# Loads of later passes in two pieces, each issued when the one in front has landed

## The chip, the cores and the metric

The kernel runs on one core of one Trainium2 chip. The metric is the device time of one execution in microseconds (us). Three runs of the kernel before gave 597.53, 600.47 and 601.56 us; the median, 600.47 us, is the time before.

## The reference

Two stages are computed. The first is a gated linear attention with a complex decay: for each of 4 x 8 heads and each of 768 steps, the decay is normalised, a 48 x 48 state is decayed and updated with the outer product of key and value, and the query reads it.

```python
scale = np.minimum(mag, 0.999) / (mag + 1e-06)      # mag = |a_re + i a_im|
for t in range(S):                                   # S = 768
    new_re = ar * S_re - ai * S_im
    new_im = ar * S_im + ai * S_re
    S_re, S_im = (new_re + einsum('bhd,bhe->bhde', k_t, v_t), new_im)
    y_t = einsum('bhd,bhde->bhe', q_t, S_re)
```

The second stage is a two-layer network on the 3072 tokens of width 384: `h = x @ w_in` (to 2048), `g = maximum(0.01 * h, h)`, `g @ w_out` (back to 384).

## The kernel before, in words

The sequence is cut into six chunks of 128 steps and the batch into two halves, which makes 12 passes (`SUBS`), each of one chunk for two batch entries, 256 tokens. A pass n has these parts:

- `fetch_a(n)` loads the decays (two planes of 128 x 768 numbers, 768 KB) into one of two buffers, `fetch_qk(n)` the queries and keys (768 KB, one buffer), `fetch_v(n)` the values (832 KB).
- `prep(n)` (lines 675 to 888) turns the decays into running products, alternating between ACT and DVE. It begins with the square of the loaded decays on ACT (the tile `sq`, read from `a`), then a DVE operation on `sq` (it is `sq<-sq` in the rows), then a logarithm and exponentials on ACT (`u`), then 14 products on DVE (`u<-a`, `a<-u`) and a scan (`xs`). Near its end it multiplies queries and keys into the tile `qkt`; that is the first use of the loaded `qk`.
- `relay_of(n, 0)` and `relay_of(n, 1)` copy `qkt` within SBUF to the tile `t96` (named `t` in the rows), five transfers each for queries and for keys.
- `attend(n)` (from line 929) computes scores, masked scores (`asb`, `more`), keys in natural order (`kn`, `more`, copied by ACT), the values' products, the rounded output `x` and its rest (ACT and DVE, both `x`), and the new state (`rst`).

`forward()` runs the network on the 256 tokens of each pass: `first` (`ph`), `hide` on ACT and DVE (`tg`, `hid`), `second` (`po`), `store`. While pass n+1 is attended, PE also has the network of the tokens of pass n. The weights are loaded and converted by `convert` while the first pass is prepared; at the end `check_weights` loads the raw weights once more in 11 parts (`wck`, up to 1152 KB each) into the two buffers of the decays and sums them on ACT for a validity test (`flag`), beside the network's last groups.

All loads and stores, and the relays, are issued by one engine, SP, in one order. That order, and the order of instructions on PE, DVE and ACT, is fixed when the kernel is built: the parts are generators that yield the engine they want next, and `drive` (line 253) takes them by modelled start time and rank, with costs from `dma_cost`, `dve_cost`, `act_cost` and `pe_costs`. The class `Lane` (line 112) chains each engine's instructions by dependencies without a semaphore, so that nothing is reordered afterwards. `fetch_a(n)` may be placed once `prep(n-2)` and the key relay of pass n-2 are placed, `fetch_qk(n)` once `prep(n-1)` and the key relay of pass n-1 are; so behind each relay of keys stand the load of the decays of two passes on and that of the queries and keys of the next pass. `prep(n)` has its first ACT instruction placed right behind the modelled landing of its decays.

Nothing makes one load wait for another, except where a buffer is reused.

Of the kernel before, what the change touches and what calls it, by code (L numbers as in the profile page):

```python
# [21 lines left out]
P = 128  # L22
# [113 lines left out]
def in_sbuf(x):  # L136
    return x.space == bass.MemoryType.SB
# [38 lines left out]
def dma_cost(name, kw, aps):  # L176
    if name == "memset":
        return 0.3, 0.4
    out = kw["out"]
    if in_sbuf(kw["in_"]) and in_sbuf(out):  # L180
        return 0.78, 2.75
    each = out.nbytes() / 400e3
    return max(each, 0.6), each + 2.4
# [272 lines left out]
def body(ctx, tc, keep, a_in, qk_in, v_in, w_in, out):  # L456
# [26 lines left out]
    spq, plq = Lane(tc, nc.sync, dma_cost), Lane(tc, nc.gpsimd, dma_cost)  # L483
# [15 lines left out]
        out=perm[:, 0].rearrange("p (x r j) -> p x r j", x=NB, r=R),  # L499
        in_=perm[:, 0].rearrange("p (x r j) -> p x r j", x=NB, r=R),  # L500
# [3 lines left out]
        out=perm[:, 1].rearrange("p (r j x) -> p r j x", r=R, j=JB),  # L504
        in_=perm[:, 1].rearrange("p (r j x) -> p r j x", r=R, j=JB),
# [28 lines left out]
    a_off = [0]  # L534
# [33 lines left out]
    def attends_of(n):  # L568
        return [attended[n]]

    def fetch_a(n):
        yield "S", *([prepared[n - 2], moved_k[n - 2]] if n > 1 else freed(A) if n else []), *([loading[n - 1]] if n else [])
        N = TI * len(SUBS[n][1]) * C
        loading[n].set(0.0)
        raw_a[n] = a = a_0 if n == 0 else pp.tile([P, 3, N], F32, tag="a", name=f"a_{n}", bufs=2)
        spq.dma_start(
            out=a[:, 1:3], in_=a_in[a_off[n] : a_off[n + 1]].rearrange("(p l x) -> p l x", p=P, l=2)
        )

    def fetch_qk(n):  # L580
        yield "S", *([prepared[n - 1], moved_k[n - 1]] if n else [])
        N = TI * len(SUBS[n][1]) * C
        raw_qk[n] = qk = pp.tile([P, 2, N], F32, tag="qk", name=f"qk_{n}")
        spq.dma_start(
            out=qk, in_=qk_in[a_off[n] : a_off[n + 1]].rearrange("(p l x) -> p l x", p=P, l=2)
        )

    def fetch_v(n):
        yield "S", *(attends_of(n - 1) if n else freed(V))
# [6 lines left out]
    def check_weights(i):  # L596
        yield "S", checked[i - 2] if i > 1 else prepared[nsub - 2 + i]
        s0 = i * WCK
        ns = min(WCK, NWC - s0)
        st = pp.tile([P, WCK, DM], I64, tag="a", name=f"wck_{s0}", bufs=2)  # L600
        spq.dma_start(out=st[:, :ns], in_=w_in[s0 : s0 + ns].rearrange("s p x -> p s x"))
        words = st.rearrange("p s x -> p (s x)").bitcast(F32).rearrange("p (x two) -> p x two", two=2)
        lo, hi = words[:, : ns * DM, 0], words[:, : ns * DM, 1]
        yield "A"
        act.activation(lo, hi, AF.Square)
        yield "A"
        act.activation(hi, lo, AF.Exp, scale=-65536.0, accum_out=wacc[:, 1, i : i + 1])
        yield "A"
        act.activation(lo, lo, AF.Exp, scale=40.0, bias=big, accum_out=wacc[:, 0, i : i + 1])

    def freed(*places):
        return [x for x, r in zip(converted, ROUND) if r in places]
# [640 lines left out]
    for n in range(nsub):  # L1253
        fetched_a[n] = task(fetch_a(n), UNIT[0] + 5.5 * UNIT[1] if n == 1 else R_RELAY + 0.5)
        fetched_qk[n] = task(fetch_qk(n), R_HID if n else UNIT[0] + 2.5 * UNIT[1])
        prepared[n] = task(prep(n), *due(n))
        if n == 0:
            for i in range(NU):
                converted.append(task(convert(i), UNIT[0] + i * UNIT[1]))
        fetched_v[n] = task(fetch_v(n), R_RELAY - 1 if n else UNIT[0] + 9.5 * UNIT[1])  # L1260
        moved_q[n] = task(relay_of(n, 0), R_RELAY)
        moved_k[n] = task(relay_of(n, 1), R_RELAY)
        attended[n] = task(attend(n), R_ATT)
    forwarding = task(forward(), R_FF)
    for i in range(-(-NWC // WCK)):
        checked[i] = task(check_weights(i), R_WCK)
# [87 lines left out]
```

## Time and profile before

| | |
|---|---|
| median of three runs | 600.47 us |
| profiled execution, its time | 598.47 us |
| profiled execution, its span | 596.5 us |
| PE, DVE, ACT busy | 92%, 88%, 65% of the span |
| chain that ended last: PE, DVE, ACT, DMA, issue | 63%, 22%, 6%, 4%, 4% |
| DMA traffic | 79.18 MB, 133 GB/s over the span |
| loads of decays; of queries and keys | 12 each, 768 KB, median 4.5 and 5.9 us from issue to landing |
| relays, 290 KB each | 48, median 4.2 us |

The span is the time from the first to the last instruction; 1.97 us of the execution lie around it. PE is TensorE, DVE VectorE, ACT ScalarE, SP the engine that issues DMAs. The chain is followed back from the last instruction, at each step to what released it; "issue" is time in which an engine waited for nothing that the profile shows. A busy share is an average over stages: whether an engine sets the pace of a stage is seen in its idle time there.

### The profile page before, as it was taken

How to read it: one execution, taken by the hardware profiler on the slowest of the kernel's cores; microseconds unless marked ns; L12 is line 12 of the kernel's file. 1: busy time of each engine (PE TensorE's matmuls, PEld its weight loads, DVE VectorE, ACT ScalarE, POOL GpSimd, SP SyncE). 2: the span in 40 equal slices, each digit the busy share in tenths (PEclk: the TensorE clock that was granted, in tenths of full speed). 3: DMA queues.
4: the chain of work that ended last, by engine and by line, in shares of the span. 5: the costliest groups of instructions: out<-in, count | busy, mean ns of one | idle time of the engine just before them, and what ended most of it. 6: DMA issues, size and time to landing. Idle time of an engine off the chain costs nothing.

```text
span 596.5 us, 17862 instructions
## 1 busy us (share of the span) xinstructions
PE 550.3 (92%) x7650; PEld 520.9 (87%) x7650; DVE 522.6 (88%) x897; ACT 388.0 (65%) x862; POOL 5.0 (1%) x23
## 2 busy tenths in 40 slices
PE   3865699999979899999999999999999999999996
PEld 2432499989869899999999999999999998998996
DVE  5999999999999999889999999999999998963332
ACT  7988576475474584584684574764755755784975
POOL 2000000000000000000000000000000000000000
PEclk9996799999999999999999999999999999999999
DMA  8963612522522433334235124134135156456650
GB/s 347 406 217 89 216 59 55 161 86 54 167 82 63 151 97 96 114 104 145 92 94 161 60 81 161 61 82 161 59 81 161 60 145 202 141 157 214 195 203 29
DMA packets 28370, 79.18 MB, mean 133 GB/s; under 512 B 3200, under 2 KB 9344, under 8 KB 28288
## 3 DMA queue, kind: packets, MB, share of 16 engines
q1 hardware_dynamic: 28288, 78.02, 40.8%
q8 instruction: 60, 0.98, 0.7%
q14 instruction: 22, 0.18, 0.1%
HBM read 54.26 MB, written 4.72 MB: 99 GB/s over the span
## 4 chain that ended last, share of the span: by engine, by line
PE 63%; DVE 22%; ACT 6%; DMA 4%; issue 4%; SPq 1%; DVEq 0%; ACTq 0%
PE ph L121 23%; PE po L121 23%; PE att L121 15%; DVE qkt L121 5%; DVE a L121 4%; DMA t<-qkt 4%; DVE u L121 3%; DVE tg L121 2%; ACT rst L121 2%; DVE hid L121 2%; DVE sq L121 1%; PE pd L121 1%; DVE xs L121 1%; DVE qk L121 1%; DMA a<-in_a_dram 1%
## 5 line engine op out<-in xcount | busy, mean ns | idle before, releaser
L121 PE MATMUL ph<-x,win_hi 128*128 128x256 f32 x1152 | 215.8, 279 | 5.2 <-DVE x L121 1.9
L121 PE MATMUL po<-hid,wout_hi 128*128 128x256 f32 x1152 | 215.1, 280 | 0.0
L121 PEld LDWEIGHTS ph<-x,win_hi 128*128 128x128 f32 x1152 | 181.4, 188 | 6.9 <-DVE x L121 2.3
L121 PEld LDWEIGHTS po<-hid,wout_hi 128*128 128x128 f32 x1152 | 180.5, 188 | 1.6 <-issue 0.4
L121 PE MATMUL ph<-x,win_lo 128*128 128x256 f32 x576 | 141.7, 278 | 0.0
L121 PE MATMUL po<-hid,wout_lo 128*128 128x256 f32 x576 | 137.2, 278 | 0.0
L121 PEld LDWEIGHTS po<-hid,wout_lo 128*128 128x128 f32 x576 | 108.4, 188 | 0.0
L121 PEld LDWEIGHTS ph<-x,win_lo 128*128 128x128 f32 x576 | 108.4, 188 | 0.0
L121 DVE TENSOR_TENSOR tg<-ph,tg 128x512 f32<-128x512 f32 x96 | 65.8, 686 | 30.6 <-ACT tg L121 30.3
L121 ACT CAST hid<-tg 128x512 fp32r<-128x512 f32 x96 | 59.3, 617 | 48.6 <-DVE tg L121 46.9
L121 ACT ACTIVATE tg<-ph 128x512 f32<-128x512 f32 x96 | 56.9, 592 | 45.4 <-PE ph L121 45.2
L121 DVE TENSOR_TENSOR hid<-tg,hid 128x512 fp32r<-128x512 f32 x96 | 65.9, 686 | 14.3 <-ACT hid L121 13.4
L121 DVE TENSOR_TENSOR u<-a 128x384 f32<-128x384 f32 x84 | 46.5, 553 | 2.1 <-ACT a L121 0.7
L121 DVE TENSOR_TENSOR qkt<-qk,a 128x768 f32<-128x768 f32 x48 | 44.1, 951 | 0.0
L121 PE MATMUL att<-t 96*32 96x64 f32 (+3 forms) x1536 | 36.0, 252 | 3.6 <-DMA t<-qkt 3.5
L121 PEld LDWEIGHTS att<-t 96*32 96x32 f32 x1536 | 33.1, 144 | 6.9 <-DMA t<-qkt 4.1
L121 PE MATMUL att<-t,rst 96*32 96x128 f32 x640 | 34.4, 272 | 1.4 <-issue 1.3
L121 PE MATMUL att<-asb,v 128*32 128x128 f32 x592 | 33.9, 274 | 0.6 <-issue 0.6
L121 ACT ACTIVATE rst<-rst,t 96x48 f32<-96x48 f32 x128 | 29.8, 322 | 4.5 <-DVE rst L121 4.4
L121 ACT ACTIVATE wck<-wck 128x1152 f32<-128x1152 f32 (+1 forms) x22 | 26.9, 1224 | 7.8 <-DMA wck<-in_w_dram 7.7
L121 DVE TENSOR_TENSOR a<-u 128x192 f32<-128x192 f32 x84 | 29.8, 355 | 1.9
L121 ACT ACTIVATE sq<-a 128x1536 f32<-128x1536 f32 x12 | 18.0, 1498 | 13.6 <-DMA a<-in_a_dram 13.6
(161 smaller groups left out, 766.9 us busy)
## 6 DMA issues: line engine op xcount, KB each, us to landing
t<-qkt SPq DMA_DIRECT2D x48, 290.2 KB, 4.2
wck<-in_w_dram SPq DMA_DIRECT2D x10, 1152.0 KB, 5.6
v<-in_v_dram SPq DMA_DIRECT2D x12, 832.0 KB, 4.5
a<-in_a_dram SPq DMA_DIRECT2D x12, 768.0 KB, 4.5
qk<-in_qk_dram SPq DMA_DIRECT2D x12, 768.0 KB, 5.9
out_dram<-ot SPq DMA_DIRECT2D x12, 384.0 KB, 2.7
t<-qkt SPq DMA_DIRECT2D x24, 129.0 KB, 4.1
stage_st<-in_w_dram SPq DMA_DIRECT2D x3, 768.0 KB, 4.4
```

Of the source, the lines that this page charges most:

```text
L121: x = getattr(self.engine, name)(*args, **kw)
```

## The change

`fetch_a` and `fetch_qk` no longer issue one transfer for the two planes of a pass, but two, one for each plane, through a new function `pieces`. Each such piece, and each part of the weight check, gets a dependency with a semaphore on the piece or part issued before it (`in_turn`): SP waits until that one has landed. The loads of pass 0 and the decays of pass 1 stay whole and outside this line, and so do the values, the relays, the stores and the weights' first load. The planner's log keeps one entry with the cost of the whole load in place of the two pieces'.

```diff
+    loaded = []
+
+    def in_turn(x):
+        if loaded:
+            landed = mybir.DependencyInfo(mybir.DependencyClass.Sync, mybir.DependencyReason.DATA)
+            tc.add_manual_dep(x.ins, loaded[-1], landed, reason="load")
+        loaded.append(x.ins.name)
+
+    def pieces(out, in_, n):
+        if n < 1:
+            spq.dma_start(out=out, in_=in_)
+            return
+        for l in range(2):
+            in_turn(spq.dma_start(out=out[:, l], in_=in_[:, l]))
+        spq.log[-2:] = [dma_cost("dma_start", dict(out=out, in_=in_), [])]
+
     def fetch_a(n):
...
-        spq.dma_start(
-            out=a[:, 1:3], in_=a_in[a_off[n] : a_off[n + 1]].rearrange("(p l x) -> p l x", p=P, l=2)
-        )
+        pieces(a[:, 1:3], a_in[a_off[n] : a_off[n + 1]].rearrange("(p l x) -> p l x", p=P, l=2), n - 1)
 
     def fetch_qk(n):
...
-        spq.dma_start(
-            out=qk, in_=qk_in[a_off[n] : a_off[n + 1]].rearrange("(p l x) -> p l x", p=P, l=2)
-        )
+        pieces(qk, qk_in[a_off[n] : a_off[n + 1]].rearrange("(p l x) -> p l x", p=P, l=2), n)
...
-        spq.dma_start(out=st[:, :ns], in_=w_in[s0 : s0 + ns].rearrange("s p x -> p s x"))
+        in_turn(spq.dma_start(out=st[:, :ns], in_=w_in[s0 : s0 + ns].rearrange("s p x -> p s x")))
```

## Rows read from the trace of the kernel before

**Rows 1.** One stretch: busy PE, PEld, DVE, ACT, POOL (instructions), granted clock, DMA, GB/s.

```profile
366.00:410.00 44.00, 44.00 (x665) 43.44 (x666) 42.35 (x73) 26.75 (x65) 0.24 (x2) 1.00 0.36 113
```

**Rows 2.** SP in order of time, one middle pass: start us, us, instruction, count.

```profile
360.85 4.00 SPq L121 DMA_DIRECT2D t<-qkt  x5
364.95 0.53 SPq L121 DMA_DIRECT2D a<-in_a_dram  x1
...
380.90 0.33 SPq L121 DMA_DIRECT2D v<-in_v_dram  x1
```

**Rows 3.** Who waited for whom, all passes: us in total, times, longest.

```profile
ACT sq L121 <- DMA a<-in_a_dram: 13.6, 11, 3.5
```

**Rows 4.** ACT in time, same pass; in brackets idle time before it.

```profile
369.23 1.49 ACT L121 ACTIVATE sq<-a 128x1536 f32<-128x1536 f32 x1 [0.77 <-DMA a<-in_a_dram]
...
372.37 0.86 ACT L121 COPY kn<-att 128x384 f32<-128x384 f32 x2 [1.56 <-PE att L121]
```

**Rows 5.** The decays' tile, all 12 loads: us from issue to landing.

```profile
DMA to landing us min/median/max: 4.3/4.5/5.3
```

**Rows 6.** DMA issues, 42.5 to 47 us: count, KB, us to landing.

```profile
stage_stg<-in_w_dram SPq DMA_DIRECT2D x1, 384.0 KB, 3.5
```

**Rows 7.** DMA issues between 60 and 64.5 us.

```profile
stage_stg<-in_w_dram SPq DMA_DIRECT2D x1, 384.0 KB, 2.9
```

**Rows 8.** DVE in order of time, the pass of Rows 4.

```profile
373.02 0.95 DVE L121 SCALAR_TENSOR_TENSOR sq<-sq 128x768 f32<-128x768 f32 x1
...
380.26 1.16 DVE L121 SCALAR_TENSOR_TENSOR x<-att,x 128x384 fp32r<-128x384 f32 x2
...
389.70 1.82 DVE L121 TENSOR_TENSOR qkt<-qk,a 128x768 f32<-128x768 f32 x2
```

**Rows 9.** The chain that ended last, same pass: start us, us, what.

```profile
381.76 2.12 PE ph L121 x18
```

**Rows 10.** ACT in order of time, the pass that loads decays at 236.92 us.

```profile
242.22 1.50 ACT L121 ACTIVATE sq<-a 128x1536 f32<-128x1536 f32 x1 [0.95 <-DMA a<-in_a_dram]
...
245.12 0.60 ACT L121 ACTIVATE tg<-ph 128x512 f32<-128x512 f32 x1 [0.57 <-PE ph L121]
```

**Rows 11.** DVE in order of time, the same pass.

```profile
243.84 0.96 DVE L121 SCALAR_TENSOR_TENSOR sq<-sq 128x768 f32<-128x768 f32 x1 [0.43 <-ACT sq L121]
...
246.59 0.53 DVE L121 TENSOR_TENSOR u<-xs 128x360 f32<-128x360 f32 x1 [0.16 <-ACT xs L121]
```

**Rows 12.** The chain that ended last, the end of that pass.

```profile
276.12 4.76 DMA t<-qkt
```

**Rows 13.** ACT in order of time, the pass that loads decays at 66.74 us.

```profile
71.31 1.49 ACT L121 ACTIVATE sq<-a 128x1536 f32<-128x1536 f32 x1 [1.25 <-DMA a<-in_a_dram]
...
74.14 0.49 ACT L121 ACTIVATE x<-att 128x384 fp32r<-128x384 f32 x1 [1.25 <-PE att L121]
```

**Rows 14.** ACT in order of time, the pass that loads decays at 196.62 us.

```profile
201.13 1.49 ACT L121 ACTIVATE sq<-a 128x1536 f32<-128x1536 f32 x1 [1.14 <-DMA a<-in_a_dram]
```

**Rows 15.** DVE in order of time, the same pass.

```profile
204.08 0.95 DVE L121 SCALAR_TENSOR_TENSOR sq<-sq 128x768 f32<-128x768 f32 x1
```

**Rows 16.** SP in order of time, parts five and six of the weight check.

```profile
540.89 1.10 SPq L121 DMA_DIRECT2D wck<-in_w_dram  x2
```

**Rows 17.** ACT in order of time: its first instruction on each part.

```profile
546.57 1.28 ACT L121 ACTIVATE wck<-wck 128x1152 f32<-128x1152 f32 x1 [4.57 <-DMA wck<-in_w_dram]
...
553.50 2.51 ACT L121 ACTIVATE wck<-wck 128x1152 f32<-128x1152 f32 x2
```

**Rows 18.** PE in order of time, the last pass.

```profile
549.78 0.31 PE L121 MATMUL att<-t,rst 96*32 96x128 f32 x3 [1.29 <-issue]
```

**Rows 19.** DMA queues, 547 to 547.5 us: packets, MB, share of engines.

```profile
q8 instruction: 1, 0.02, 12.7%
```

**Rows 20.** Who waited for whom, all passes: PE's waits in the attention.

```profile
PE att L121 <- DMA t<-qkt: 3.5, 6, 1.1
...
PE att L121 <- issue: 2.6, 3, 1.3
```

## The prediction

> **What bounds the kernel now.** I read the page's chain first, then busy time by stretch, then SP's order, then the engines' own orders around each load. In the middle passes PE has no idle time at all: 44.00 us busy in a stretch of 44 us [rows 1]. There an edit to the loads can only cost time, or free PE from something that the profile books as busy. The five passes whose decays are issued between 279 and 451 us look like this; the five split passes before them do not, and there DVE and ACT are on the chain.
>
> In SP's order the load of the decays stands right behind the five transfers of a key relay, and the queries and keys right behind it; the next thing on SP, the load of the values, is issued 16 us later (380.90 - 364.95) [rows 2]. What the reader should see next is that the decays are not loaded far ahead: in 11 of 12 passes ACT waits for them, 13.6 us in total [rows 3]. ACT takes the square as soon as they land, and then has 1.56 us to spare before its copy of the keys [rows 4]. So the landing time of the decays is what the change moves and what someone waits for.
>
> **The change, part by part.** Order and count on PE, DVE and ACT: unchanged, since the planner is given the same cost and the same order. Issues: 10 passes of decays and 11 of queries and keys get one more, 21 in all, at 0.53 us of SP each [rows 2]. SP has 16 us free there, so their own issue time costs nothing.
>
> *Landing of the decays.* Whole, they land 4.5 us after issue, 4.3 to 5.3 [rows 5]. A piece is 384 KB. The trace has transfers of just this size: 3.5 us with relay transfers about [rows 6], 2.9 us later on with less beside it [rows 7]. The first piece follows the key relay, so I take 3.5; the second is alone in the queue, so 2.9; between them a wake-up of SP, which I take as 0.05. Together 6.45 us, 1.95 later than now. Ends: two quick pieces against the median give 2 x 2.9 + 0.05 - 4.5 = 1.35; two slow ones 2.55; and since half a load should not take longer than the whole at its slowest, at the most 2 x 5.3 - 4.5 = 6.1. No gain is possible here: two transfers one after the other would have to land in 2.25 us each, and no row of this size is below 2.9.
>
> The Trainium skill ("DMA: Bandwidth & Descriptors", Anatomy of one DMA) speaks against the change: each transfer has a fixed part of about 2.0 us, beside bytes at 436 GB/s. By it a piece would be 2.9 us as an estimate, a whole 3.8, the delay 2.0, and the sum below the same to 0.1 us; the 2.9 agrees with the row, the whole is slower here.
>
> *Middle passes, five.* The square ends at 369.23 + 1.49 = 370.72 us [rows 4]; DVE reads it at 373.02 [rows 8]. Slack 2.3 us; the other four have 2.1 to 2.4 by the same two rows. Further on, DVE's last step on the output ends at 380.26 + 1.16 = 381.42 [rows 8] and PE takes it no earlier than 381.76 [rows 9], so 0.34 us more. A delay of 1.95 fits: **0**. ACT's copy of the keys slips by 1.95 - 1.56 = 0.4 us at most [rows 4]; behind it ACT idles again before PE wants anything. The cover is gone when the delay passes about 2.6 us; then each us beyond costs up to five.
>
> *The pass at 236.92 us.* Here there is no slack: DVE already waits 0.43 us for the square [rows 11]. ACT's next piece of the network idled only 0.57 us [rows 10], between them the key copy follows the square directly. So tg slips by 1.95 - 0.57 = about 1.4, DVE's scan behind ACT's copies by the same 1.4 [rows 11], and the chain goes on over DVE and ACT without a break to the key relay that releases PE at 280.9 [rows 12]. **+1.4**; ends 0 and 1.95.
>
> *The pass at 196.62 us.* The square ends at 202.62 [rows 14], DVE reads it at 204.08 [rows 15]: slack 1.46, so DVE stalls 0.5. PE is busy behind, with some room: **+0.4**. The two passes before it have like slack (both are on DVE's chain); I charge 0.15 each: **+0.3**, ends 0 and 1.
>
> *The pass at 66.74 us.* The square's end moves from 72.8 to 74.75; ACT's output step is due at 74.14 [rows 13]. It slips by 0.6 us. How much reaches PE no row shows; I take all but a part: **+0.5**, ends 0 and 0.6.
>
> *Queries and keys.* Their pieces follow those of the decays: 364.95 + 6.45 + 3 x 0.05 + 2 x 2.9 = 377.3 us at the last landing. DVE reads them at 389.70 [rows 8] and SP's next issue is at 380.90 [rows 2], so they cost **0**; 3.4 us remain to SP, and if the pieces took 1 us more each it would still do. Where a store of results stands next in SP's order (two early passes), it is the store that slips, and nobody waits for it.
>
> *Weight check.* Parts five and six are issued one right after the other now [rows 16]; five lands at 546.57 and is used at once, six is used at 553.50 [rows 17]. In line, six is issued at 546.6 and takes again 546.57 - 540.89 = 5.7 us at most [rows 16], so it lands at 552.3, in time: **0**. The later parts wait for ACT to free their buffer already.
>
> *What it could give back.* In the last pass PE waits 1.29 us with nothing that the profile names [rows 18]; shortly before, a packet of its instructions passes among the data of those two parts [rows 19]. I read this as code that came late behind a bulk load. With one part in flight at a time the queue is shorter. There are 2.6 us of such waits on PE in three places [rows 20]; one more of them stands at a load of decays, one behind a single part that stays whole. I take **-1.0**, ends 0 and -2.6. The Trainium skill ("Runtime: NRT & Kernel Launch", Instruction fetch mechanics) has instruction fetch mostly hidden. By it the credit would be 0 and the time 1 us longer; the row of 1.29 us does not fit it, though no row proves what the wait was for.
>
> **Sum.** 1.4 + 0.4 + 0.3 + 0.5 - 1.0 = +1.6 us against the profiled execution's 598.47. That one lies 2.0 us under the median of the runs and inside their spread; the mean of all four is 599.5. I forecast 599.5 + 1.6 = **601 us**, which a measurement cannot tell from no change: about 1% (6 us) is what it can tell here.
>
> **Rivals.**
> *Slower: the slack of the middle passes is overrun.* The place is DVE's read of the square [rows 8], the mechanism the in-order wait of ACT for the second piece, the point 2.6 us of delay. If the pieces take 4.1 us each, about what a whole load takes now, the delay is 3.75: then 5 x 1.15 = 5.8 in the middle and 1.8 more in each of the five early passes, 9 us, atop +2.6: 599.5 + 17 = 617. At 3.1 us of delay it is 2.5 + 5.8 + 2.6 = 11, so 610. For it: the first piece shares the engines with a relay. Against: both rows of this size are below 3.6 [rows 6, 7]. Chance 0.22, with the time most likely 607 to 611.
>
> *Faster: PE was held up by loads more than I credit.* If all of PE's named waits in the attention, 3.5 us for relays and 2.6 us for nothing named [rows 20], went, and the delay cost nothing, it would be 599.5 - 6.1 = 593.4. Against: the relays are issued ahead of the loads [rows 2], and shorter loads behind them do not speed them. Chance 0.10.
>
> *The change does nothing.* Were the wait met before SP comes to it, or the decays' landing unchanged, the time would be 599.5. Against: the second piece comes 0.5 us after the first, which cannot have landed. Chance 0.08.
>
> **How the numbers follow.** Forecast 0.60. The forecast's own range is 597 to 604, from -1.0 to -2.6 of credit below and all upper ends of the four charges above. The whole range runs from 596, into the faster case, to 608, into the lower half of the slower one; outside lie about 0.07 and 0.11. Slower by over 1% (above 606.5): most of the slower rival, 0.19. Faster by over 1% (under 594.5): the stronger part of the faster one, 0.06. Within 1%: 0.75.
>
> **What would show it.** In the profile after: decays landing some 6.4 us after their first issue, the second piece's issue about 3.5 us behind the first; ACT's waits for decays up from 13.6 to about 33 us; PE still without idle in the middle passes; DVE waiting for the square in the early passes only; the 1.29 us wait of the last pass smaller or gone. I am wrong if pieces land much sooner or later than 2.9 to 3.5 us, if DVE waits for the square in every pass, or if PE is found to run faster in stretches that show it fully busy now.

## The result: about 1% slower, and the profile after

The changed kernel takes 605.53 us (median of six runs), the kernel before 599.96 beside it; the ratio is 1.0109, with a 95% interval of 1.0064 to 1.0155. That is 5.6 us of loss where 1.6 were forecast. The time lies 4.5 us above the forecast, above the forecast's own range (597 to 604) and inside the whole one (596 to 608); the ratio is just past 1%, with an interval that reaches to both sides of it. The profiled executions differ by as much: 603.8 against 598.47 us. One run of all, 608.18 us in the experiment with whole decays, fell in a slower state of the chip and is left out of the medians and ratios.

The page of the kernel after: span, busy time, clock by slice, the chain that ended last, and the loads among the DMA issues (count, KB each, us to landing).

```profile
span 602.1 us, 17917 instructions
...
PE 550.5 (91%) x7650; PEld 520.9 (87%) x7650; DVE 522.8 (87%) x897; ACT 386.0 (64%) x862; POOL 5.0 (1%) x23
...
PEclk9896789999999999999999999999999999999999
...
DVE 50%; ACT 17%; PE 13%; DMA 12%; issue 5%; SPq 2%; ACTq 0%; DVEq 0%
...
qk<-in_qk_dram SPq DMA_DIRECT2D x22, 384.0 KB, 3.2
a<-in_a_dram SPq DMA_DIRECT2D x20, 384.0 KB, 3.3
```

No engine works longer: PE and DVE are busy for the same time as before, to 0.2 us, in a span 5.6 us longer. What changed is the chain, from PE 63% to DVE 50%, with ACT and DMA behind it. The added time is waiting.

Who waited for whom (us in total, times, longest), the rows that answer to [rows 3, 20] and the one behind them:

```profile
ACT sq L121 <- DMA a<-in_a_dram: 38.1, 11, 5.8
DVE tg L121 <- ACT tg L121: 28.9, 24, 3.9
ACT tg L121 <- PE ph L121: 17.8, 22, 2.8
...
DVE sq L121 <- ACT sq L121: 11.7, 8, 4.1
...
PE att L121 <- DMA t<-qkt: 4.5, 10, 1.5
...
PE att L121 <- ACT win_lo L121: 3.2, 1, 3.2
...
PE att L121 <- issue: 2.0, 3, 1.1
```

ACT waits 24.5 us more for the decays than before. Its waits for PE are shorter (`ACT tg <- PE ph` was 45.2 us and is 17.8), so I read that time which ACT had in hand is spent; the row scatters, though: it is 26.5 when the changed kernel is run again, and 27.9 in a kernel whose decays land as before (the first experiment). DVE's wait for ACT's square was 5.5 us in three places and is 11.7 in eight; two of the eight, 4.1 and 1.04 us, stand in both kernels. So 6.2 us of DVE waits are new, about the loss.

SP in order of time, the pass of [rows 2], now issued 6.76 us later in the span:

```profile
367.56 4.05 SPq L121 DMA_DIRECT2D t<-qkt  x5
371.71 3.58 SPq L121 DMA_DIRECT2D a<-in_a_dram  x2
378.26 3.40 SPq L121 DMA_DIRECT2D qk<-in_qk_dram  x2
386.99 0.33 SPq L121 DMA_DIRECT2D v<-in_v_dram  x1
```

The second piece goes out some 3.2 us behind the first (the pair ends at 375.29 and its last issue takes about 0.3), and the queries only when it has landed, 6.55 us after the start. The values are issued 386.99 - 371.71 = 15.3 us after the decays, where it was 16, so they are not held up.

The decays' tile, all 22 transfers (two whole, 20 pieces), against [rows 5]:

```profile
DMA to landing us min/median/max: 3.0/3.3/5.0
```

Three stretches of 44 us, the middle passes (columns as in [rows 1]), and in them one pass on ACT and DVE in order of time, the load at 285.83 us; below it the same two instructions before, the load at 279.50 us:

```profile
284.00:328.00 44.00, 43.37 (x665) 42.78 (x664) 42.29 (x73) 27.14 (x67) 0.12 (x1) 1.00 0.39 108
328.00:372.00 44.00, 43.91 (x671) 43.33 (x669) 42.17 (x73) 26.70 (x66) 0.12 (x1) 1.00 0.38 108
372.00:416.00 44.00, 43.80 (x705) 43.06 (x707) 42.63 (x74) 26.37 (x65) 0.12 (x1) 1.00 0.38 108
```

```profile
292.82 1.49 ACT L121 ACTIVATE sq<-a 128x1536 f32<-128x1536 f32 x1 [3.56 <-DMA a<-in_a_dram]
294.22 0.18 ACT L121 ACTIVATION_READ_ACCUMULATOR sq<-a 128x1 f32 x1
294.31 0.84 ACT L121 COPY kn<-att 128x384 f32<-128x384 f32 x2
```

```profile
294.43 0.96 DVE L121 SCALAR_TENSOR_TENSOR sq<-sq 128x768 f32<-128x768 f32 x1 [0.52 <-ACT sq L121]
```

```profile
283.85 1.49 ACT L121 ACTIVATE sq<-a 128x1536 f32<-128x1536 f32 x1 [0.93 <-DMA a<-in_a_dram]
```

```profile
287.48 0.95 DVE L121 SCALAR_TENSOR_TENSOR sq<-sq 128x768 f32<-128x768 f32 x1
```

Here the slack is gone: ACT starts the square 6.99 us after the first issue, where it was 4.35, and DVE stands still for 0.52 us, where it came 2.14 us after the square's end. The copy of the keys follows the square without idle time, which [rows 4] have in another middle pass. PE is no longer busy in every microsecond.

The pass that had no slack, answering to [rows 11], and the wait of the last pass, answering to [rows 18]:

```profile
250.84 0.96 DVE L121 SCALAR_TENSOR_TENSOR sq<-sq 128x768 f32<-128x768 f32 x1 [2.19 <-ACT sq L121]
```

```profile
555.31 0.31 PE L121 MATMUL att<-t,rst 96*32 96x128 f32 x3 [1.13 <-issue]
```

And the first split pass, which lost most. Chain (start us, us, what), ACT, PE, and two windows:

```profile
66.83 3.37 DMA a<-in_a_dram
70.19 0.02 issue
70.21 5.00 DMA a<-in_a_dram
```

```profile
75.32 1.48 ACT L121 ACTIVATE sq<-a 128x1536 f32<-128x1536 f32 x1 [5.17 <-DMA a<-in_a_dram]
...
77.72 0.48 ACT L121 CAST win_lo<-att 128x384 fp32r<-128x384 f32 x1
```

```profile
78.25 0.55 PE L121 MATMUL att<-ident,t 96*128 96x96 f32 x4 [3.23 <-ACT win_lo L121]
...
80.02 0.41 PE L121 MATMUL ph<-x,win_hi 128*128 128x256 f32 x1
```

```profile
76.00:80.00 4.00, 1.75 (x7) 1.24 (x8) 3.01 (x6) 3.06 (x9) 0.00 (x0) 0.87 0.53 117
80.00:84.00 4.00, 4.00 (x29) 3.87 (x29) 3.51 (x11) 1.81 (x5) 0.00 (x0) 0.71 0.21 84
```

The second piece took 5.00 us. Behind it on ACT, in order, stand the outputs `x` and then a weight conversion (`win_lo`) that PE reads; PE waited 3.23 us for it, 0.59 before. After that idle time the granted clock, 1.00 at this place in the kernel before, was 0.87 and then 0.71, part of the time at the lower of its two levels (1.2 instead of 2.4 GHz): the network's product takes 0.41 us instead of 0.28.

### The profile page after: what moved, and what is told of

It is laid out like the page before. It is cut to its first block, busy times and chain, and to the rows that moved or that the text cites. A ratio compares the mean times of both kernels' runs of the same rounds, so it can differ in the third digit from the quotient of the medians.

```text
span 602.1 us, 17917 instructions
## 1 busy us (share of the span) xinstructions
PE 550.5 (91%) x7650; PEld 520.9 (87%) x7650; DVE 522.8 (87%) x897; ACT 386.0 (64%) x862; POOL 5.0 (1%) x23
## 4 chain that ended last, share of the span: by engine, by line
DVE 50%; ACT 17%; PE 13%; DMA 12%; issue 5%; SPq 2%; ACTq 0%; DVEq 0%
DVE qkt L121 10%; DVE a L121 9%; DVE tg L121 7%; DVE u L121 7%; DVE hid L121 6%; DMA a<-in_a_dram 5%; ACT rst L121 4%; PE ph L121 4%; PE att L121 4%; PE po L121 3%; DVE sq L121 3%; ACT a L121 2%; DVE xs L121 2%; DMA t<-qkt 2%; DMA wck<-in_w_dram 2%
## 5 line engine op out<-in xcount | busy, mean ns | idle before, releaser
L121 ACT ACTIVATE tg<-ph 128x512 f32<-128x512 f32 x96 | 57.0, 594 | 19.0 <-PE ph L121 17.8
L121 DVE TENSOR_TENSOR qkt<-qk,a 128x768 f32<-128x768 f32 x48 | 44.1, 952 | 0.0
L121 ACT ACTIVATE sq<-a 128x1536 f32<-128x1536 f32 x12 | 17.9, 1490 | 38.1 <-DMA a<-in_a_dram 38.1
```

Of the source, the lines that this page charges most:

```text
L121: x = getattr(self.engine, name)(*args, **kw)
```

## The experiments

Each edit is to the changed kernel; every kernel computes the whole result. "DVE's wait" is the row `DVE sq <- ACT sq`, in total. Ratios are to the kernel before, run beside each, with 95% intervals.

**Only the decays whole again** (queries, keys and weight check stay as changed):

```diff
-        pieces(a[:, 1:3], a_in[...], n - 1)
+        pieces(a[:, 1:3], a_in[...], 0)
```

> The loads of decays are whole again and out of the line; queries and keys in two pieces and the weight check stay in line. Theory (the whole loss is the later landing of the decays, which ACT waits for in order): ratio to the kernel before 1.000, between 0.996 and 1.004; decays land 4.3 to 5.3 us after issue, ACT's waits for them back near 14 us. Rival A (the line of weight parts and of queries and keys costs, SP being held by waits of 57 us for decays and 35 us for queries and keys): ratio 1.004 to 1.010. Rival B (code fetches come sooner when loads are short): ratio 0.994 to 0.998.

600.54 against 598.89 us: 1.0027 (1.0001 to 1.0052). DVE's wait is 5.7 us, ACT's for the decays 14.3. Most of the loss goes with the decays; the 0.3% that is left is taken up further down.

**Only the decays in two pieces**:

```diff
-        pieces(qk, qk_in[...], n)
+        pieces(qk, qk_in[...], 0)
-        in_turn(spq.dma_start(out=st[:, :ns], ...))
+        spq.dma_start(out=st[:, :ns], ...)
```

> Only the loads of decays are in two pieces in line; queries and keys are whole and the weight check is out of the line. Theory: the same loss as the changed kernel, ratio to before 1.007 to 1.014; the square starts 6.5 to 7 us after the first issue (a little later than in the changed kernel where the whole load of queries and keys cannot be in front, so the same). Rival A (line of the others): ratio 1.000 to 1.004.

605.51 against 598.89: 1.0114 (1.0079 to 1.0148). DVE's wait 11.9 us, ACT's 38.1. The decays alone bring the whole loss.

**Pieces, but none waits for another**:

```diff
-        if loaded:
+        if False:
```

> The pieces stay, two transfers for each load, but none waits for another and the weight check doesn't either. Theory (the wait between the pieces costs, not the second transfer): the decays land 4.3 to 5.3 us after the first issue, ratio 0.998 to 1.004. Rival C (two transfers are dear by themselves, by SP's issue time or by their number): decays land over 6 us after the first issue, ratio 1.006 or more.

601.41 against 598.89: 1.0040 (1.0015 to 1.0065). Its waits:

```profile
ACT sq L121 <- DMA a<-in_a_dram: 13.7, 11, 3.5
...
DVE sq L121 <- ACT sq L121: 5.1, 2, 4.1
```

Both as before the change. Two transfers in place of one do not delay the square; the wait between them does, and most of the loss goes with it. The 0.4% that is left is taken up further down.

**First split pass whole, the nine later ones split**:

```diff
-        pieces(a[:, 1:3], a_in[...], n - 1)
+        pieces(a[:, 1:3], a_in[...], n - 2)
```

> As the changed kernel, but the decays of pass 2, the first that were split, stay whole. In the profile of the changed kernel events run 3.7 us late from that pass on and about 2 us more come in the rest. Theory D (most of the loss is in that one pass, whose second piece took 5.0 us and where PE waited for ACT): ratio 1.002 to 1.006. Rival E (what is lost early is taken up later, the middle passes being paced by DVE's stalls): ratio 1.008 to 1.012, as the changed kernel.

602.21 against 598.89: 1.0065 (1.0041 to 1.0090), between what the two theories gave it. DVE's wait is 9.6 us, PE's for `win_lo` back at 0.6. Some part of the loss stands in the first split pass, and about as much or more in the later ones.

**Only the first split pass in pieces**, the converse:

```diff
-        pieces(a[:, 1:3], a_in[...], n - 1)
+        pieces(a[:, 1:3], a_in[...], int(n == 2))
-        pieces(qk, qk_in[...], n)
+        pieces(qk, qk_in[...], 0)
-        in_turn(spq.dma_start(out=st[:, :ns], ...))
+        spq.dma_start(out=st[:, :ns], ...)
```

> Only the decays of pass 2, the first that were split, are in two pieces in line; all other loads are as before. Theory D (that pass is worth about half of the loss, PE stalling behind ACT's weight copy, as leaving it whole gave back 0.5%): ratio 1.003 to 1.007, PE's wait for ACT in that pass 2.5 to 3.3 us against 0.59. Rival E (taken up later): ratio 1.000 to 1.002.

600.53 against 598.65: 1.0023 (0.9990 to 1.0056), less than I expected, and not distinguished from no change. In its profile the square came 6.57 us after the issue, and PE waited 0.59 us for `win_lo`, as before the change: the long second piece did not come up.

**Decays in four pieces of 192 KB, in line** (queries and keys whole, weight check out of the line): the same wait, three times instead of once.

```diff
-            in_turn(spq.dma_start(out=out[:, l], in_=in_[:, l]))
-        spq.log[-2:] = [...]
+            for h in range(2):
+                x = slice(h * 384, h * 384 + 384)
+                in_turn(spq.dma_start(out=out[:, l, x], in_=in_[:, l, x]))
+        spq.log[-4:] = [...]
```

> The loads of decays in four pieces in line (half a plane each), queries and keys whole, the weight check out of the line: the wait before ACT's square doubled. Theory (ACT's square, then DVE's read of it, wait in order; slack 2.3 us in the middle passes, as before): the decays land near 4 x 3 = 12 us after the first issue, 7.5 us later than before, DVE waits about 5 us for the square in every pass, ten passes: 35 to 55 us more, ratio 1.06 to 1.09. Rival F (only the first split pass pays and the middle passes hide any delay behind ACT's idle time): ratio 1.01 to 1.03.

642.78 against 598.65: 1.0736 (1.0689 to 1.0784), as expected of the delay. Its pieces land in 2.4 us at the median. Its waits:

```profile
ACT sq L121 <- DMA a<-in_a_dram: 71.9, 11, 9.9
...
DVE sq L121 <- ACT sq L121: 45.3, 12, 5.7
...
PE att L121 <- ACT kn L121: 22.7, 9, 4.5
```

Past the slack every pass pays: DVE's wait grows by 39.8 us, the time by 44. Now ACT's copy of the keys is late for PE as well, nine times.

**The planner told the later landing** (pieces and waits as changed):

```diff
-        spq.log[-2:] = [dma_cost("dma_start", dict(out=out, in_=in_), [])]
+        spq.log[-2:] = [(6.6, 6.8)]
```

> The changed kernel, but the planner's log has 6.6 us of SP and 6.8 us to landing for two pieces (in place of 2.0 and 4.4), near what they take. The order of instructions on ACT and DVE then moves. Theory (the loss is an order planned for a landing 2.3 us sooner): ACT's waits for decays fall from 38 us to under 20, DVE's waits for the square under 7, ratio to before 1.000 to 1.005. Rival G (the delay costs in any order, since the pass has no room for it): ratio 1.007 to 1.014.

612.55 against 598.65: 1.0224 (1.0184 to 1.0263). A miss for the theory and for its rival: the waits fell as I had said, and the kernel became slower still.

```profile
DVE qkt L121 <- issue: 10.2, 3, 3.4
...
DVE sq L121 <- ACT sq L121: 5.7, 3, 4.4
...
DVE scr L121 <- ACT wck L121: 5.1, 1, 5.1
...
ACT sq L121 <- DMA a<-in_a_dram: 3.9, 2, 2.9
```

```profile
497.00:543.00 46.00, 41.50 (x551) 40.05 (x550) 40.23 (x68) 24.64 (x45) 0.12 (x1) 1.00 0.50 151
```

With another landing time the planner wrote another order for all engines; DVE now stands at its products and at the weight check's end, and PE is idle for 4.5 us in 46 near the end, 1.3 in the stretch of before that answers to it. Which step of the new order costs what was not followed further. So a small wait for the square alone is no proof of a fast kernel; the link between this wait and the time holds for one order only.

**Whole loads, in line** (queries and keys wait for the decays, nothing is cut, weight check out of the line):

```diff
-        for l in range(2):
-            in_turn(spq.dma_start(out=out[:, l], in_=in_[:, l]))
-        spq.log[-2:] = [...]
+        in_turn(spq.dma_start(out=out, in_=in_))
+        spq.log[-1:] = [...]
-        in_turn(spq.dma_start(out=st[:, :ns], ...))
+        spq.dma_start(out=st[:, :ns], ...)
```

> Loads whole, but queries and keys are issued only when the decays in front of them have landed; weight check as before. It keeps the part of the change by which loads don't share the engines, without the second piece. Theory: the decays land 3.9 to 4.4 us after issue, a little sooner than the 4.5 before, ratio 0.996 to 1.002; if the first, it would be better than both. Rival B (code fetches are helped by fewer bytes in flight): 0.990 to 0.996.

601.40 against 598.65: 1.0043 (1.0012 to 1.0073), a miss: no better than before, perhaps worse. Its loads:

```profile
a<-in_a_dram SPq DMA_DIRECT2D x12, 768.0 KB, 4.5
qk<-in_qk_dram SPq DMA_DIRECT2D x12, 768.0 KB, 4.3
```

The decays land in 4.5 us at the median, as before, though the queries and keys no longer follow them into the queue. It is the queries and keys that land sooner, 4.3 us instead of 5.9, and nobody waits for those. So keeping this company away from the decays had nothing to give.

**Everything undone**, with the kernel before's own instructions, to see what the comparison itself gives:

```diff
-        pieces(a[:, 1:3], a_in[...], n - 1)
+        pieces(a[:, 1:3], a_in[...], 0)
-        pieces(qk, qk_in[...], n)
+        pieces(qk, qk_in[...], 0)
-        in_turn(spq.dma_start(out=st[:, :ns], ...))
+        spq.dma_start(out=st[:, :ns], ...)
```

> Every part of the change undone, with its functions left in the file: the instructions of the kernel before. It says what the comparison itself gives where nothing differs. Ratio 0.998 to 1.002 if the 0.3 to 0.4% of the three kernels whose decays land as before is a real cost; if it is 1.002 to 1.005 here too, that 0.3% is the comparison's own.

599.83 against 600.04: 0.9995 (0.9966 to 1.0024). The comparison has no offset of its own. But the profile's span is 600.6 us where that of before is 596.5, so two profiles of the same instructions differ by 4 us; a pass of a single profile proves little. Of these 4 us, 1.9 stand in one pass, where PE idled 1.54 us and the granted clock was then 0.57 for 4 us (below).

**Only the weight check in line**, run twice; the second label is the same kernel:

```diff
-        pieces(a[:, 1:3], a_in[...], n - 1)
+        pieces(a[:, 1:3], a_in[...], 0)
-        pieces(qk, qk_in[...], n)
+        pieces(qk, qk_in[...], 0)
```

> Only the weight check's parts are in line; all other loads are as before. Theory (free, since ACT takes each part later than it lands in line): ratio 0.998 to 1.002. Rival B: below 0.998 by code fetches, PE's 1.29 us wait of the last pass gone; rival A: 1.002 to 1.005, the line delaying the end.

> The weight check's parts in line and nothing else, once more: the only part of the change whose middle value lay below 1 (0.9983, interval 0.9957 to 1.0010). Theory (free): 0.997 to 1.002 again, PE's wait in the last pass smaller than the 1.29 us of before. Rival B (a real gain by code fetches): interval wholly below 1.

598.08 against 600.04, 0.9983 (0.9957 to 1.0010); and 598.42 against 599.44, 0.9993 (0.9964 to 1.0022). The line costs the weight check nothing, and a gain is not shown. No version beats the kernel before by more than its interval. In both profiles PE's wait of the last pass [rows 18] is missing; what is left of its waits for nothing named stands elsewhere. The first of the two:

```profile
PE att L121 <- issue: 1.0, 2, 0.6
```

```profile
547.43 0.51 PE L121 MATMUL att<-t,rst 96*32 96x128 f32 x6
```

So the wait went, as rival B had said; the gain that it expected from this is not shown.

**The changed kernel again**, unedited:

> The changed kernel once more, beside the two others on one chip, and a second profile of it. Theory: ratio 1.007 to 1.013; the first split pass shows again a second piece of 4.5 to 5 us and a stall of PE behind ACT's weight copy of 2.5 us or more. If the piece lands in 3.0 to 3.5 us and PE does not stall there, that part of the loss comes and goes, and the ratio nevertheless holds by the other passes.

604.88 against 600.04: 1.0078 (1.0050 to 1.0107). DVE's wait 11.7 us again. In its profile the first split pass had an ordinary second piece:

```profile
73.69 1.48 ACT L121 ACTIVATE sq<-a 128x1536 f32<-128x1536 f32 x1 [3.59 <-DMA a<-in_a_dram]
```

```profile
76.63 0.55 PE L121 MATMUL att<-ident,t 96*128 96x96 f32 x4 [0.62 <-ACT win_lo L121]
```

The 3.23 us wait of PE and the low clock behind it belong to one execution, not to the change in every run; the loss is there without them.

## Why the prediction was right and wrong

The number first. 605.53 us lies outside the forecast's own range and inside the whole one, whose upper part was drawn from the slower rival; and a part of the loss came in that rival's way, at DVE's read of the square in the middle passes. There is some luck in how near the total came: one charge was about twice too large, and several were too small.

The main mechanism stood: the decays land later, ACT's square waits for them in order, DVE waits for the square. With the order of instructions as it is in the change, DVE's wait for the square in the profile goes with the time lost in the runs:

| kernel | DVE's wait, us more than the 5.5 of before | time, us more than before |
|---|---|---|
| changed; again; decays only | 6.2; 6.2; 6.4 | 5.6; 4.8; 6.6 |
| first split pass whole | 4.1 | 3.3 |
| decays in four | 39.8 | 44.1 |
| pieces without wait; decays whole; whole in line; first pass only | -0.4; 0.2; 0.4; 0.2 | 2.5; 1.7; 2.8; 1.9 |
| weight check in line, twice; undone | 0.3; 0.0; 0.1 | -2.0; -1.0; -0.2 |

*Landing of the decays: the term was too small.* Pieces land in 3.3 us at the median; I had 3.5 for the first and 2.9 for the second. By place, the first piece took 3.33 us and the second 3.34 in the profile after: the second is no faster for being alone in the queue. SP's wake-up between them, taken as 0.05, was 0.02 (the row `issue` of the chain above). From the first issue to the square it was 6.38 to 8.49 us (median 6.7) in the ten split passes of the profile after, against 4.27 to 5.30 (median 4.5) before; pass by pass 1.5 to 2.9 later, 3.9 in the first, median 2.2, where the forecast was 1.95. The step that failed is "the second is alone in the queue, so 2.9": it rested on a single row [rows 7], and it gave one number for a delay that scatters. ("No row of this size is below 2.9" overlooked the stores of results, 384 KB in 2.7 us at the median; the conclusion stands, since the pieces took 3.0 us and more.) The Trainium skill ("DMA: Bandwidth & Descriptors", Anatomy of one DMA) has a fixed part of about 2.0 us in each transfer, by which a piece of 384 KB would be 2.9 and one of 192 KB 2.45 as estimates. Its fit was taken on transfers issued by GpSimd, which the prediction did not say; the ones here are issued by SP. The traces agree for the small one (2.4) and give 0.4 us more for the other (3.3). Going from 768 to 384 to 192 KB, 4.5, 3.3 and 2.4 us, a halving of the bytes never came near to halving the time, and that is the rule that spoke against this change.

*Where the time went, pass by pass.* From one load of the decays to the next in SP's order, in profiles of four kernels that load them whole (before, undone, weight check in line twice) and of three that split them (changed, decays only, changed again); the passes are named by their issue in the kernel before:

| from the load at | whole, us | split, us | forecast | read as |
|---|---|---|---|---|
| 66.7 | 42.93 to 42.97 | 46.51, 44.87, 43.33 | +0.5 | +0.4 to +3.6 |
| 109.7 | 44.65 to 45.08 | 45.43, 45.25, 45.24 | +0.15 | +0.5 |
| 154.4 | 42.14 to 42.27 | 42.20, 42.22, 42.23 | +0.15 | 0 |
| 196.6 | 40.30, 40.31, 40.81, 43.13 | 41.48, 40.91, 41.62 | +0.4 | +0.9 |
| 236.9 | 42.58, 42.66, 42.85, 44.45 | 43.38, 43.40, 44.05 | +1.4 | +0.7 |
| 279.5, three passes | 126.95 to 128.38 | 128.29, 128.87, 131.22 | 0 | 0 to +3 |
| 407.4 to the last store | 183.29 to 186.10 | 183.67, 184.22, 186.52 | -1.0 | 0 |

Three figures are left out of the readings: 43.13, 44.45 and 44.05. In each of those profiles the granted clock was 0.57 to 0.58 for 4 or 8 us of that pass, with PE busy throughout; in the kernel before it was 1.00 there. Two of the three kernels load the decays whole, so this comes without the change too. (Such stretches also fell into the passes at 109.7 and 154.4 in three of these profiles and left no mark there.) The stretches of the first two (columns as in [rows 1]):

```profile
198.00:206.00 8.00, 8.00 (x142) 7.80 (x143) 7.69 (x18) 2.57 (x5) 0.12 (x1) 0.57 0.56 199
```

```profile
240.00:244.00 4.00, 4.00 (x91) 3.85 (x81) 3.43 (x9) 1.95 (x3) 0.02 (x1) 0.57 0.77 301
```

Without them the means of the columns (42.95 and 44.90 in the first line) differ by 2.0, 0.5, 0.0, 0.9, 0.7, 1.7 and 0.2 us, about 6 us in all (with them the fourth and fifth would be 0.2 and 0.5, and the sum 5); the runs of these split kernels lost 4.8 to 6.6. The forecast had +1.6. Three terms make the difference: the first split pass, the middle passes and the credit. The errors of the others, of both signs, cancel.

*The pass at 66.74 us, +0.5 forecast.* In the quiet case it is that (0.4, changed again); in two of three profiles the second piece took 4.7 to 5.0 us, PE waited 2.64 and 3.23 us for `win_lo`, and it was +1.9 and +3.6. The 1.6 us between these two are about what the low clock took: the two stretches shown above lost 4 x 0.13 + 4 x 0.29 = 1.7 us of it, and in the other profile it was 1.00 there. The reach to PE, which "no row shows", was ACT's order: the conversion that PE reads stands behind the square too. My upper end of 0.6 was wrong, since it took a delay of 1.95 as the most there could be.

*Middle passes, 0 forecast.* The slack was read rightly (2.1 to 2.5 us; I wrote 2.4). In the profile after two of the five overran it: delays of 2.64 and 2.87 us against slacks of 2.1 and 2.2, and DVE stalled 0.52 and 0.68 us. With only the decays in pieces it was three of five, in the changed kernel run again four, and there one load took 8.88 us and DVE stood 1.80. What I had as a rival from 2.6 us on, all or none, is crossed by single passes at a delay whose median is 2.2. I weighed the slack against a mean; the scatter decided.

*The credit of -1.0 us.* It did not come. The wait of the last pass went from 1.29 to 1.13 us, 1.17 when run again, and all such waits on PE from 2.6 to 2.0 and 3.0 us in total. With nothing but the weight check in line the wait was gone, in two profiles of two, and the medians lay 2.0 and 1.0 us under the kernel before, within the noise. With the weight check in line and the queries and keys in pieces (decays whole) it was 1.67, and in the undone kernel 1.30. So the line alone does not decide over this wait, and a gain by it is neither shown nor excluded. The Trainium skill ("Runtime: NRT & Kernel Launch", Instruction fetch mechanics), which has instruction fetch mostly hidden, gave a credit of 0; the times agree with that to within the noise, though no run shows what the 1.29 us was for.

*The pass at 236.92 us, +1.4 forecast.* DVE's stall went from 0.43 to 2.19, 1.8 us more; the pass became 0.7 us longer. The stall is in the rows; that most of it reaches the end was the error. Where it was taken up was not followed.

*What held.* Queries and keys: split or not, behind split decays, 1.0109 and 1.0114. Weight check 0. Issue time on SP: with pieces and no wait the square came 4.25 to 4.84 us after the first issue, no later than whole. ACT's wait for decays, forecast at about 33 us, is 38.1, since the pieces are slower. "DVE waiting for the square in the early passes only" was wrong by the middle passes above.

*Left open.* The kernels with whole or early decays, but queries and keys in pieces or in line (decays whole, pieces without wait, whole in line), lie at 1.0027 to 1.0043 with intervals that just leave out 1, and DVE's wait is not longer in them. In the undone kernel the same comparison gives 0.9995. So handling queries and keys so may cost up to 0.4%; with split decays the same edit shows nothing (1.0109 against 1.0114 without it). What it would be was not found. A lead is the granted clock: its mean over the runs is 0.977, 0.977 and 0.975 in these three, and 0.980, 0.980 and 0.979 in the runs of before beside them (undone and before beside it: 0.979 and 0.978). As an estimate, 0.003 to 0.004 of 600 us are 1.8 to 2.4 us, about what is open. Decays only and changed again have a lower clock too (0.975 against 0.980, 0.976 against 0.978), so some of their loss may come the same way. Whether the lower clock costs the time or comes of PE's added idle time is not shown.

## What to carry to other kernels

A load that someone waits for in every pass is not made earlier by cutting it and putting a wait between the halves: here the halves landed one after the other, and each took three quarters of the time of the whole (3.3 of 4.5 us). Set the later landing against the slack of each pass separately, and against its scatter, not its median; passes whose slack is about as large as the delay already cost time. Before a pass is compared between two profiles, look at the granted clock in it: stretches at 0.57 were worth more here than the effect looked for. And follow the engine that waits in order: what stands behind the waiting instruction on ACT (here a weight conversion for PE) is late as well, whatever it is.

## What the runs showed of the hardware

The second of two pieces sometimes took far longer than its twin: 5.00 us after 3.37 in the first split pass. The tail of it, 73.0 to 74.9 us, on the DMA queues:

```profile
DMA packets 9, 0.02 MB, mean 13 GB/s; under 512 B 1, under 2 KB 1, under 8 KB 9
```

Nine packets in 1.9 us, with nothing else on the queues: the transfer was not short of bandwidth, its last packets came one at a time. Why was not found. It came in two of the five profiles with this pass in two pieces (4.7 us in the kernel with only the decays in pieces), and in other passes too: 5.13 us in a middle pass of the changed kernel run again.

After PE's idle time of 3.23 us the granted clock was 0.87 and 0.71 in the two stretches shown above; after one of 2.64 us at the same place, in the kernel with only the decays in pieces, it stayed at 1.00. Elsewhere like idle time came with either clock. From 194 to 198 us PE idled 1.83 us in the second profile with the weight check in line and 1.82 in the kernel before; from 198 to 206 us the clock was 0.57 in the one and 1.00 in the other. What decides it was not found.
